# Linear attention feeding an MLP on one core: in which batch k is loaded, and where kv joins the numerators

## The chip, the cores and the metric

The kernel runs on one core of one Trainium2 chip. The metric is device time in microseconds (us), the median of several runs. The engines are named as in the profile: PE is TensorE (matrix products), PEld its weight loads, DVE is VectorE, ACT is ScalarE, POOL is GpSimd, SP is SyncE, which here only issues transfers. Each engine works through its own instructions in program order; engines wait for each other and for transfers (DMA) through semaphores.

## The reference

For 8 batches of 8 heads, 576 positions and head size 64, with phi(x) = elu(x) + 1:

```python
q_p, k_p = phi(q), phi(k)
kv  = einsum('bhsd,bhse->bhde', k_p, v)
z   = sum(k_p, axis=2)
num = einsum('bhsd,bhde->bhse', q_p, kv)
den = einsum('bhsd,bhd->bhs', q_p, z)[..., None] + 1e-06
attn = num / den
# heads side by side: x is 4608 x 512
h = x @ w_in                      # 512 -> 2048
g = h / (1 + exp(-beta * h))
out = g @ w_out                   # 2048 -> 512
```

All inputs and the output are float32. The kernel converts to bf16 on load or in the engines.

## The kernel before, in words

Each batch has nine rows of 64 positions (J = 9) per head. Eight of them make four tiles of 128 positions for the MLP; the ninth, the odd one, goes with the odd rows of all other batches into a last block, xT_tail. So the MLP runs nine times over 512 positions: b = 0 to 7 for the batches and b = 8 for the tail.

One MLP pass has two phases. `h_phase(b)` makes 16 groups (FC = 16): each is four matmuls `x @ w_in` into one PSUM bank (L454, in h_mm) and one silu on ScalarE that writes g (L462). The banks come from `mmps`, a pool of four; a fifth group can start only when the first silu has read its bank. `y_phase(b)` makes four tiles of 128 positions: 16 matmuls each (L472, in y_mm), a copy to SBUF on VectorE (L245) and two stores (L487).

The attention of later batches is laid between these matmuls by hand. Two dictionaries, `sh` and `sy`, hold for each pass what is emitted after group ff of the h phase and after quarter 4t + i of the y phase; `at(sh, 8, f)` adds f after group 8. In the pass b, n = b + 1 is the batch whose x is made ready, and m = b + 2 the one whose phi is made. The emission order is the order in which every engine executes its share, so an instruction that must wait holds up all later ones of its engine.

The pieces, with their profile lines:

- `load_q`, `load_k` (L83) are issued by GpSimd; `load_v` (L83) by SP. Inputs rotate over three buffers (xq, xk: batch mod 3) or two (vf). `load_q(b, after)` is held until the transfer `after` has landed: this is the DMA transpose of phi(q) of the batch before, so that the loads don't take the queues from it. What GpSimd has behind a held load waits too.
- `phi_exps` runs two exps on ScalarE (L144), one for each pair of heads; `phi_rest` the max and the min on VectorE (L148, L155); `phi_all` both. Exp and Silu are in different tables, so each change between them is an ACT_TABLE_LOAD.
- `v_copies` (L173, GpSimd) puts v as bf16 beside a column of ones.
- kv is 72 small matmuls (L184). `kv_both(b)` gives them a PSUM tile of their own (from numps, two buffers) and one copy to SBUF (L239). `numers(b, after)` makes the numerators and denominators of batch b (L309), divides (norms, L392 and L383), and with `after` set first puts kv of batch `after` into free columns of the same PSUM tiles and copies it at the end (L342).
- `q_trans_dma` (L275), `x_trans_dma` (L442 for the four tiles, L446 for the odd row) are transposes by DMA, issued by SP. The first matmul of a h phase needs all four of x.
- `q_odd_trans` (L284) transposes the odd row of phi(q) of batches 0 and 1 on TensorE and copies it on ScalarE (L288). In the pass b = 1 its PSUM tile comes from numps, and the two groups 3 and 4 of that pass also use tiles of numps.

In the kernel before, in the pass b = 1, k of batches 3 and 4 are both loaded early in the h phase, k of batch 5 in the y phase; phi(k) of batch 3 is made in the y phase, and the exps of k of batch 4 at its end. From the pass b = 2 on one pattern holds: kv of batch m goes with `numers(n, m)`, its phi_rest and v_copies are in the h phase, and the exps of the k after it are at step 10 of the y phase.

Of the kernel before, what the change touches and what calls it, by code (L numbers as in the profile page):

```python
# [9 lines left out]
BF16 = mybir.dt.bfloat16  # L10
# [6 lines left out]
def kernel(  # L17
# [12 lines left out]
    B, H, S, D = q.shape  # L30
# [4 lines left out]
    FC = DFF // P  # L35
# [44 lines left out]
    def load(eng, dst, src, b, h0=0, n=4):  # L80

        rows = src[b].rearrange("h (g j) d -> (h g) (j d)", j=J)
        return eng.dma_start(  # L83
            out=dst[:, h0 : h0 + n].rearrange("p h j d -> p h (j d)"),
            in_=rows.rearrange("(i p) e -> p i e", p=P)[:, h0 : h0 + n],
        )
# [84 lines left out]
    def v_copy(eng, b, pr):  # L171
        src = vb[b % 2] if b == 2 else vf[b % 2]
        eng.tensor_copy(  # L173
            vaug[b % 2][:, pr, :, :, 0:D], src[:, places(b, pr)].rearrange("p h j d -> p j h d")
        )
# [51 lines left out]
    def num_tile(name):  # L227
        return numps.tile([P, 2, 512], F32, tag="num", name=name)

    def kv_pair(b, pr, dst):  # L230
        k_quads(b, pr, dst, lambda r, j, h: vaug[b % 2][r, pr, j, h, 0:EA])

    def kv_both(b):

        t = num_tile("kvp")
        for pr in range(2):
            kv_pair(b, pr, [t[:, hh, pr * EA : (pr + 1) * EA] for hh in range(2)])
        st[b, "kvd"] = work.tile([P, 2, 2 * EA], BF16, tag="kv_bd", name="kvd")
        nc.vector.tensor_copy(st[b, "kvd"], t[:, :, 0 : 2 * EA])  # L239
# [40 lines left out]
    def q_odd_trans(b, tp):  # L280

        tv = tp.rearrange("p (a n) -> p a n", a=2)
        for pr in range(2):
            nc.tensor.matmul(  # L284
                tv[:, pr], st[b, "q"][:, pr, J - 1, :], identity,
                is_transpose=True, start=True, stop=True, skip_group_check=True,
            )
        nc.scalar.copy(  # L288
            q_odd[b].rearrange("p (i a) g -> p a i g", i=2),
            tv.rearrange("p a (i g) -> p a i g", i=2),  # L290
        )
# [11 lines left out]
    def quads(b, dst, e, stat, hh, pr):  # L303

        for c in range(2):
            p, j = stat(c)
            for h in range(2):
                r = slice(h * D, (h + 1) * D)
                nc.tensor.matmul(  # L309
                    dst[h][c * G : (c + 1) * G, e * EA : (e + 1) * EA],  # L310
                    st[b, "qTd"][r, (hh * 2 + p) * J + j, :],
                    st[b, "kvd"][r, hh, p * EA : (p + 1) * EA],
                    start=True, stop=True, skip_group_check=True,
                )

    def numer_tile(b, dst, t, prs=(0, 1), e0=0):
        for pr in prs:
            for hh in range(2):
                e = e0 + 2 * (pr - prs[0]) + hh
                quads(b, dst, e, lambda c, pr=pr: (pr, 2 * t + c), hh, pr)  # L320

    def numers(b, after=None):

        pairs = [num_tile("nps") for _ in range(2)]
        odd = [mm_tile("nps_m") for _ in range(2)]
        if after is not None:
            for pr in range(2):
                kv_pair(after, pr, [pairs[pr][:, hh, 6 * EA : 7 * EA] for hh in range(2)])
        for k in range(2):
            dst = [pairs[k][:, h] for h in range(2)]  # L330
            numer_tile(b, dst, k)
            numer_tile(b, dst, 2, (k,), 4)
        numer_tile(b, odd, 3)
        for hh in range(2):
            quads(b, odd, 4 + hh, lambda c: (c, J - 1), hh, None)
        st[b, "nps"] = pairs, odd
        for k in range(3):
            norms(b, k)
        if after is not None:
            st[after, "kvd"] = work.tile([P, 2, 2 * EA], BF16, tag="kv_bd", name="kvd")  # L340
            for pr in range(2):
                nc.vector.tensor_copy(  # L342
                    st[after, "kvd"][:, :, pr * EA : (pr + 1) * EA],
                    pairs[pr][:, :, 6 * EA : 7 * EA],
                )
# [39 lines left out]
    def norms(b, k):  # L385

        den = work.tile([P, 2, 6], F32, tag="den", name="den")
        rden = work.tile([P, 2, 6], F32, tag="rden", name="rden")
        pairs, odd = st[b, "nps"]
        if k < 2:  # L390
            nv = pairs[k][:, :, 0 : 6 * EA].rearrange("p h (n e) -> p h n e", e=EA)
            nc.vector.tensor_scalar(den, nv[:, :, :, D], 1e-6, None, ALU.add)  # L392
            nc.vector.reciprocal(rden, den)
            x = xs_tile(b, k).rearrange("p (h n) d -> p h n d", h=2)
            scale(x, nv[:, :, 0:4, 0:D], rden[:, :, 0:4])
            if k == 0:
                xs_tile(b, 2)
            x = st[b, "xs", 2].rearrange("p (h n) d -> p h n d", h=2)
            scale(x[:, :, 2 * k : 2 * k + 2], nv[:, :, 4:6, 0:D], rden[:, :, 4:6])
            return  # L400
        nv = [a[:, 0 : 6 * EA].rearrange("p (n e) -> p n e", e=EA) for a in odd]
        for h in range(2):
            nc.vector.tensor_scalar(den[:, h], nv[h][:, :, D], 1e-6, None, ALU.add)
        nc.vector.reciprocal(rden, den)
        x = xs_tile(b, 3)
        for h in range(2):
            scale(x[:, 4 * h : 4 * h + 4], nv[h][:, 0:4, 0:D], rden[:, h, 0:4])
        x = xs_tile(b, 4)
        for h in range(2):
            scale(x[:, 2 * h : 2 * h + 2], nv[h][:, 4:6, 0:D], rden[:, h, 4:6])  # L410
# [55 lines left out]
    def mm_tile(name):  # L466
        return mmps.tile([P, 512], F32, tag="mm", name=name)
# [21 lines left out]
    def load_q(b, after):  # L489
        if b < B:  # L490
            hold(load(nc.gpsimd, xq[b % NX], q, b), after)

    def load_k(b):
        if b < B:
            load(nc.gpsimd, xk[b % NX], k, b)

    def load_v(b):
        if b < B:
            load(nc.sync, vf[b % 2], v, b)

    def phi_exps(b, a):
        for pr in range(2):
            phi_part(b, a, pr, xin(b, a, pr))

    def phi_rest(b, a):
        phi_tile(b, a)
        for pr in range(2):
            phi_relu(b, a, pr, xin(b, a, pr))
        for pr in range(2):
            phi_min(b, a, pr)  # L510

    def phi_all(b, a):
        phi_exps(b, a)
        phi_rest(b, a)

    def v_copies(b):
        for pr in range(2):
            v_copy(nc.gpsimd, b, pr)
# [318 lines left out]
    def at(side, n, *fs):  # L837
        side.setdefault(n, []).extend(fs)
# [3 lines left out]
    for b in range(1, B + 1):  # L842
        n = b + 1
        m = n + 1
        sh, sy = {}, {}
        if b == 1:
            at(sh, 0, lambda: q_trans_dma(2))
            at(sh, 1, lambda: v_copies(2))
            at(sh, 2, lambda: load_q(3, st[2, "qTd", "dma"]), lambda: load_k(3))
            at(sh, 2, lambda: load_v(3), lambda: load_k(4))  # L850
            at(sh, 6, lambda: q_odd_trans(1, num_tile("qop")[:, 0].bitcast(BF16)[:, 0:256]))
            at(sh, 8, lambda: kv_both(2))
            at(sy, 1, lambda: numers(2))
        elif n < B:
            if b == 2:
                at(sh, 8, odd_numers, odd_norms, lambda: kv_both(3))
                at(sh, 9, lambda: [x_trans_dma(i, 4) for i in range(2)])
            if m < B:
                at(sh, 2, lambda: phi_rest(m, "k"))
                at(sh, 6, lambda: v_copies(m))  # L860
            at(sh, FC - 1, lambda: numers(n, m if m < B else None))
        if n < B:
            for t in range(NT):
                at(sy, t // 3 + (2 if b == 1 else 0), lambda t=t: x_trans_dma(n, t))
        if m < B:
            at(sy, 3, lambda: phi_all(m, "q"))
            at(sy, 5, lambda: q_trans_dma(m), lambda: load_q(m + 1, st[m, "qTd", "dma"]))
            at(sy, 5, lambda: load_k(m + 2))
            if b == 1:
                at(sy, 4, lambda: v_copies(3))  # L870
                at(sy, 8, lambda: phi_all(3, "k"))
            at(sy, 9, lambda: load_v(m + 1))
            if m + 1 < B:
                at(sy, 10, lambda: phi_exps(m + 1, "k"))
        h_phase(b, xT[b % 3] if b < B else xT_tail, sh)
        y_phase(b, sy, last=(b == B))
# [30 lines left out]
```

## Time and profile before

| | before |
|---|---|
| median of 3 runs | 285.83 us (285.32 to 286.75) |
| span of the profiled execution | 285.3 us |
| TensorE busy | 275.2 us (96%) |
| ScalarE busy | 160.6 us (56%) |
| VectorE busy | 107.8 us (38%) |
| GpSimd busy | 37.3 us (13%) |
| mean over the span | 144 GB/s in 51723 packets |

Busy time counts the instructions' own durations, matmul ends are modelled, and a busy share over the whole span doesn't say where an engine waits. In the timeline, the pass b = 1 begins its h phase at about 49 us and its y phase at 64; the pass b = 2 at 80 and 97; the pass b = 3 at 110.5 and 126. A row gives start, length, engine, line, operation, output and input, the number of instructions merged (x4), and in brackets how long the engine was idle before and what ended that. A wait for several semaphores is put down to the one that came last by the profile, which can name the wrong one. SPq is SP's issuing of transfers.

### The profile page before, as it was taken

How to read it: one execution, taken by the hardware profiler on the slowest of the kernel's cores; microseconds unless marked ns; L12 is line 12 of the kernel's file. 1: busy time of each engine (PE TensorE's matmuls, PEld its weight loads, DVE VectorE, ACT ScalarE, POOL GpSimd, SP SyncE). 2: the span in 40 equal slices, each digit the busy share in tenths (PEclk: the TensorE clock that was granted, in tenths of full speed). 3: DMA queues.
4: the chain of work that ended last, by engine and by line, in shares of the span. 5: the costliest groups of instructions: out<-in, count | busy, mean ns of one | idle time of the engine just before them, and what ended most of it. 6: DMA issues, size and time to landing. Idle time of an engine off the chain costs nothing.

```text
span 285.3 us, 5983 instructions
## 1 busy us (share of the span) xinstructions
PE 275.2 (96%) x2482; PEld 139.1 (49%) x2512; DVE 107.8 (38%) x260; ACT 160.6 (56%) x219; POOL 37.3 (13%) x51
## 2 busy tenths in 40 slices
PE   7799999999989999999999999999999999999994
PEld 2574457444834544454445444544444444444443
DVE  5832578806732464037403840281025100110012
ACT  4878586973776942785288617831860186028500
POOL 8732100314013000320040003000000000000000
PEclk9999999999999999999999999999999999999999
DMA  7999999489969829983997369335403510230032
GB/s 217 205 213 390 249 262 224 109 190 233 199 137 288 141 65 162 269 153 67 162 276 126 80 155 274 56 80 136 99 3 79 117 37 0 57 80 12 0 74 75
DMA packets 51723, 41.03 MB, mean 144 GB/s; under 512 B 31584, under 2 KB 43120, under 8 KB 51696
## 3 DMA queue, kind: packets, MB, share of 16 engines
q1 hardware_dynamic: 38800, 23.61, 34.5%
q0 software_dynamic: 12736, 16.91, 30.1%
q8 instruction: 19, 0.31, 0.5%
q10 hardware_dynamic: 160, 0.13, 0.2%
q14 instruction: 8, 0.07, 0.1%
HBM read 36.71 MB, written 9.44 MB: 162 GB/s over the span
## 4 chain that ended last, share of the span: by engine, by line
PE 91%; DMA 3%; POOL 1%; ACT 1%; issue 1%; DVE 0%; POOLq 0%; ACTq 0%
PE y_ps L472 44%; PE h_ps L454 41%; DMA w_in<-in_moe_w_in_dram 3%; PE nps L184 1%; PE h_ps L665 1%; ACT g L462 1%; PE nps L309 1%; POOL vf L83 1%; PE kvp L184 0%; PE nps_m L309 0%; POOL xk L83 0%; PE nps L563 0%; PE nps L265 0%; PE tp L655 0%; PE zt L194 0%
## 5 line engine op out<-in xcount | busy, mean ns | idle before, releaser
L462 ACT ACTIVATE g<-h_ps,beta_c 128x512 bf16<-128x512 f32 x144 | 97.8, 689 | 89.2 <-PE h_ps L454 88.8
L472 PE MATMUL y_ps<-w_out,g 128*128 128x512 bf16 (+4 forms) x621 | 126.5, 359 | 0.9 <-issue 0.2
L454 PE MATMUL h_ps<-xT,w_in 128*128 128x512 bf16 x486 | 108.5, 379 | 1.9 <-DVE r L148 1.3
L472 PEld LDWEIGHTS <-g 128*128 128x128 bf16 x636 | 60.9, 98 | 61.1
L454 PEld LDWEIGHTS <-w_in 128*128 128x128 bf16 x560 | 54.4, 98 | 66.5 <-issue 1.7
L245 DVE COPY y_sb<-y_ps 128x512 f32<-128x512 f32 (+2 forms) x37 | 24.9, 673 | 81.1 <-PE y_ps L472 81.1
L392 DVE TENSOR_SCALAR den<-nps 128x12 f32<-128x12 f32 x12 | 2.0, 165 | 63.5 <-PE nps L309 63.5
L144 ACT ACTIVATE e<-xk 128x1152 bf16<-128x1152 bf16 x16 | 17.8, 1153 | 2.3 <-DMA xk<-in_k_dram 2.3
L83 POOL DMA_DIRECT2D xq<-in_q_dram x7 | 5.2, 748 | 90.4 <-DMA qTd<-phi_q 44.8
L144 ACT ACTIVATE e<-xq 128x1152 bf16<-128x1152 bf16 x14 | 15.6, 1155 | 0.1
L454 PE MATMUL h_ps<-xT_tail,w_in 128*128 128x512 bf16 x62 | 13.9, 379 | 0.1
L173 POOL CAST vaug<-vf 128x1152 bf16<-128x1152 f32 x10 | 11.2, 1148 | 18.0 <-DMA vf<-in_v_dram 13.5
L155 DVE TENSOR_TENSOR phi_q<-e,r 128x1152 bf16<-128x1152 bf16 (+2 forms) x17 | 11.7, 719 | 2.7 <-ACT e L144 2.4
L155 DVE TENSOR_TENSOR phi_k<-e,r 128x1152 bf16<-128x1152 bf16 x16 | 12.5, 808 | 0.1
L383 DVE TENSOR_TENSOR xs<-nps,rden 128x512 bf16<-128x512 f32 (+1 forms) x24 | 12.3, 552 | 0.4
L144 ACT ACT_TABLE_LOAD x6 | 7.7, 1283 | 6.7 <-DMA xq<-in_q_dram 6.7
L133 PE MATMUL warm_ps<-xT 128*128 128x512 bf16 x20 | 7.5, 530 | 1.8 <-DVE xT L96 1.5
L462 ACT ACT_TABLE_LOAD x6 | 7.7, 1283 | 0.1
L83 POOL DMA_DIRECT2D xk<-in_k_dram x9 | 6.8, 757 | 4.5 <-DMA g<-in_moe_w_out_dram 1.8
L148 DVE TENSOR_SCALAR r<-xq 128x1152 bf16<-128x1152 bf16 x14 | 6.8, 520 | 1.0 <-DMA xq<-in_q_dram 1.0
L184 PEld LDWEIGHTS <-phi_k 64*64 64x64 bf16 x576 | 5.6, 106 | 3.1 <-issue 2.1
L730 DVE TENSOR_SCALAR w_out<-g,rbeta 128x512 bf16<-128x512 f32 x8 | 3.8, 537 | 8.2 <-DMA g<-in_moe_w_out_dram 8.2
(98 smaller groups left out, 119.5 us busy)
## 6 DMA issues: line engine op xcount, KB each, us to landing
out_dram<-y_sb SPq DMA_DIRECT2D x70, 128.0 KB, 2.5
vf<-in_v_dram SPq DMA_DIRECT2D x5, 1152.0 KB, 6.4
xq<-in_q_dram POOLq DMA_DIRECT2D x7, 576.0 KB, 10.0
xk<-in_k_dram POOLq DMA_DIRECT2D x7, 576.0 KB, 12.4
w_in<-in_moe_w_in_dram POOLq DMA_DIRECT2D x4, 512.0 KB, 12.5
g<-in_moe_w_out_dram POOLq DMA_DIRECT2D x2, 1024.0 KB, 17.4
stage<-in_moe_w_out_dram POOLq DMA_DIRECT2D x2, 1024.0 KB, 20.5
stage<-in_q_dram SPq DMA_DIRECT2D x2, 576.0 KB, 4.4
```

The source lines that it names most:

```text
L83: return eng.dma_start(out=dst[:, h0 : h0 + n].rearrange("p h j d -> p h (j d)"), in_=rows.rearrange("(i p) e -> p i e", p=P)[:, h0 : h0 + n],
L133: nc.tensor.matmul(warm_ps[:, 0:cols], warm[:, 0:P], warm[:, 0:cols], start=True, stop=True)
L144: nc.scalar.activation(st[b, a, pr, "e"][:, :, j0:j1], x[:, :, j0:j1], ACTF.Exp)
L148: nc.vector.tensor_scalar(r, x, 0.0, 1.0, ALU.max, ALU.add)
L155: nc.vector.tensor_tensor(st[b, a][:, pr, j0:j1].rearrange("p j (h d) -> p j h d", h=2), st[b, a, pr, "e"][:, :, j0:j1].rearrange("p h j d ...
L173: eng.tensor_copy(vaug[b % 2][:, pr, :, :, 0:D], src[:, places(b, pr)].rearrange("p h j d -> p j h d"))
L184: nc.tensor.matmul(dst[hh][c], st[b, "k"][r, pr, j, c], mov(r, j, h), start=(j == 0), stop=(j == J - 1), skip_group_check=True,)
L245: eng.tensor_copy(dst, src)
L383: nc.vector.tensor_mul(out, num, rd[..., None].to_broadcast(list(num.shape)))
L454: nc.tensor.matmul(hp[:, c0:c1], w_in_sb[ff // 4][:, kc, (ff % 4) * P : (ff % 4 + 1) * P], x[:, kc, c0:c1], start=(kc == 0), stop=(kc == K ...
L462: nc.scalar.activation(g_sb[b % 2][:, ff, :], hp, ACTF.Silu, scale=beta_c[:, ff : ff + 1])
L472: nc.tensor.matmul(yp[:, c0:c1], g_sb[b % 2][:, ff, t * P : (t + 1) * P], w_out_sb[i][:, c, c0:c1], start=(ff == 0), stop=(ff == FC - 1), ...
```

## The change

kv of batch 4 gets a kv_both of its own in the h phase of the pass b = 3, in place of a share of numers(3) in the pass b = 2; the pattern with `after` holds from batch 5 on. k of batch 4 is loaded in the y phase of the pass b = 1 behind q of batch 4, in place of the h phase of that pass; its phi and v_copies go to the y phase of the pass b = 2. It is for a lighter load on the DMA queues in the pass b = 1, where x of batch 2 is transposed. The load of k of batch 5 is now in the pass b = 2, behind q of batch 5; its exps stay at step 10 of that pass's y phase. The odd row of phi(q) of batch 1 is transposed after group 7 in place of group 6.

```diff
@@ the pass b = 1, h phase
-            at(sh, 2, lambda: load_v(3), lambda: load_k(4))
-            at(sh, 6, lambda: q_odd_trans(1, num_tile("qop")[:, 0].bitcast(BF16)[:, 0:256]))
+            at(sh, 2, lambda: load_v(3))
+            at(sh, 7, lambda: q_odd_trans(1, num_tile("qop")[:, 0].bitcast(BF16)[:, 0:256]))
@@ n < B, b > 1
-            if m < B:
+            if b == 3:
+                at(sh, 8, lambda: kv_both(4))
+            if 4 < m < B:
                 at(sh, 2, lambda: phi_rest(m, "k"))
                 at(sh, 6, lambda: v_copies(m))
-            at(sh, FC - 1, lambda: numers(n, m if m < B else None))
+            at(sh, FC - 1, lambda: numers(n, m if 4 < m < B else None))
@@ m < B
             at(sy, 3, lambda: phi_all(m, "q"))
             at(sy, 5, lambda: q_trans_dma(m), lambda: load_q(m + 1, st[m, "qTd", "dma"]))
-            at(sy, 5, lambda: load_k(m + 2))
-            if b == 1:
-                at(sy, 4, lambda: v_copies(3))
-                at(sy, 8, lambda: phi_all(3, "k"))
+            if b < 3:
+                at(sy, 5, lambda: load_k(m + 1))
+                at(sy, 4, lambda: v_copies(m))
+                at(sy, 8, lambda: phi_all(m, "k"))
+            if b > 1:
+                at(sy, 5, lambda: load_k(m + 2))
             at(sy, 9, lambda: load_v(m + 1))
-            if m + 1 < B:
+            if 4 < m + 1 < B:
                 at(sy, 10, lambda: phi_exps(m + 1, "k"))
```

## The prediction

> **What bounds the kernel now.** I read the busy shares on the page first, then TensorE's waits, then the timeline around each wait and around the place where the change puts work, and last the times to landing of the transfers concerned. Page, parts 1 and 4:
>
> ```profile
> PE 275.2 (96%) x2482; PEld 139.1 (49%) x2512; DVE 107.8 (38%) x260; ACT 160.6 (56%) x219; POOL 37.3 (13%) x51
> ...
> PE 91%; DMA 3%; POOL 1%; ACT 1%; issue 1%; DVE 0%; POOLq 0%; ACTq 0%
> ```
>
> TensorE sets the end: nothing is won but by removing its gaps, and any new gap is lost in full. The view of who waited for whom, TensorE alone, has two gaps after the first 15 us:
>
> ```profile
> PE h_ps L454 <- DVE r L148: 1.3, 1, 1.3
> ...
> PE qop L284 <- ACT g L462: 0.4, 1, 0.4
> ```
>
> The timeline shows where they are, and what engines do at the start of batch 3's h phase (columns: start, length, then what, with the idle time before it in brackets):
>
> ```profile
> 1.46 5.92 PE L133 MATMUL warm_ps<-xT 128*128 128x512 bf16 x15 [1.46 <-DVE xT L96]
> ...
> 52.99 4.16 ACT L462 ACTIVATE g<-h_ps,beta_c 128x512 bf16<-128x512 f32 x7
> ...
> 55.47 0.27 PE L284 MATMUL qop<-identity,phi_q 128*128 128x128 bf16 x2 [0.39 <-ACT g L462]
> ...
> 73.89 1.66 SPq L442 DMA_TRANSPOSE xT<-xs  x1
> ...
> 80.33 7.93 PE L454 MATMUL h_ps<-xT,w_in 128*128 128x512 bf16 x35 [1.25 <-DVE r L148]
> ...
> 95.24 0.85 PE L184 MATMUL nps<-vaug,phi_k 64*64 64x65 bf16 x72
> ...
> 99.47 2.20 ACT L144 ACTIVATE e<-xk 128x1152 bf16<-128x1152 bf16 x2
> ...
> 101.69 1.28 ACT L462 ACT_TABLE_LOAD   x1
> ...
> 107.78 2.80 SPq L275 DMA_TRANSPOSE qTd<-phi_q  x2
> ...
> 110.50 13.98 PE L454 MATMUL h_ps<-xT,w_in 128*128 128x512 bf16 x63
> 111.56 0.69 ACT L462 ACTIVATE g<-h_ps,beta_c 128x512 bf16<-128x512 f32 x1 [8.59 <-PE h_ps L454]
> ...
> 114.51 0.75 POOL L83 DMA_DIRECT2D xq<-in_q_dram  x1 [22.22 <-ACT g L462]
> 115.25 0.76 POOL L83 DMA_DIRECT2D xk<-in_k_dram  x1
> ```
>
> See in it: the exps of k of batch 5 run at 99.47, eleven microseconds before ScalarE is needed again at 111.56; and the loads of q of batch 5 and k of batch 6 are issued at 114.51 and 115.25, after batch 3's h phase has begun. That is harmless here, because what they bring is wanted a batch later. Times to landing, first of the x transpose issued at 73.89, then of the k load issued at 115.25:
>
> ```profile
> DMA to landing us min/median/max: 6.4/6.4/6.4
> ```
>
> ```profile
> L83 POOL DMA_DIRECT2D xk<-in_k_dram x1: 760/760/760, 115.2 to 115.2; - x1
> DMA to landing us min/median/max: 12.1/12.1/12.1
> ```
>
> The first corrects a name: 73.89 + 6.4 = 80.29, and TensorE starts at 80.33. The gap of 1.25 us put down to DVE's r is a wait for the last transpose of x of batch 2. In later batches the same transposes land 2.3 us after issue; here k of batches 3 and 4 fills the queues (their loads, issued at 63.6 and 64.4, land at about 72.7 and 76.8).
>
> **What the Trainium skill says.** "DMA: Bandwidth & Descriptors", "Queues, rings and completion order": descriptors of one queue row are consumed in ring order, and an engine takes turns between rows. The trace agrees: q3, k3 and k4, issued 0.75 us apart from GpSimd, land in that order at 69.2, 72.7 and 76.8, and transposes from the other queue get slow beside them. "Perfetto Trace Analysis", "Tensor Engine Instruction": ScalarE, VectorE and GpSimd are strict FIFOs. The trace agrees in that no engine's order departs from the source. "ScalarE: Activation LUTs", "What ACT_TABLE_LOAD costs": 1283 ns for the load; the trace has 1.28 us. "TensorE: Matmul & The Clock Gate", "What's actually happening": after about 3.4 us idle TensorE goes to half clock until it has been busy for about as long. The trace's granted clock shows 1.00 throughout, but the first 15 warm-up matmuls take 5.92 us, 0.39 us each, against 13.8 us for 64 (0.216 each) in an h phase; so it fits.
>
> **The change part by part.**
> 1. q_odd_trans one group later. Its transpose waits until the fourth silu of batch 1 is done: ScalarE starts these at 52.99 and goes on every 0.59, so it is done at 55.47, and TensorE had been ready since 55.08. After the change group 7 (0.86 us) runs first, its bank free since the second silu, and the transpose comes at about 55.95, with nothing to wait for. ScalarE's 0.41 us copy lies beside matmuls. Gain 0.4.
> 2. k of batch 4 no longer loaded at 64.4. Its last share of the queues (72.7 to 76.8) falls away, so the last x transpose, issued near 73.5, lands between 2.3 us (later batches) and about 5 us later, at 75.8 to 78.5; TensorE wants it at 79.07 - 0.39 = 78.7. Gain 1.25, or 1.65 with part 1. ScalarE also drops two exps and VectorE four operations there; both are off the path.
> 3. k of batch 4 is now loaded behind q of batch 4, exactly where k of batch 5 was (issued 85.37, landed 13.5 later, 98.9). Its exps come at the eighth step of batch 2's y phase, after those of q at 97 to 99.5. In time.
> 4. kv of batch 4: 72 small matmuls (0.78 in the chain) leave the numerators of batch 3 and come back after group 8 of batch 3's h phase (0.64 for the like of batch 3). Net -0.1; one VectorE copy in place of two is hidden.
> 5. k of batch 5. This is the part that counts. The old code loads it in batch 1 (m + 2 = 5). The new code has, in batch 1, load_k(4) alone, and in batch 2 load_k(5), both after load_q; but the exps of k of batch 5 stay at the tenth step of batch 2's y phase. So load_k(5) stands on GpSimd behind load_q(5), which is held until the transpose of phi(q) of batch 4 has landed. That is the 114.51 of the trace, and k5 takes the place that k6 had at 115.25. On ScalarE the two exps of k5 stand ahead of the table load and of all silus of batch 3.
>    The working: all that leads to 114.51 follows batch 3's numerators (VectorE's xs, four x transposes, two tail transposes, two stores, the qTd transposes, back to back on the SP queue), and moves earlier by 1.65 (parts 1, 2) + 0.78 (part 4) = 2.43. q5 is issued at 112.08, k5 0.74 later at 112.82. Nothing shows k5 itself here, so I take k6's 12.1 us to landing, the same place beside the same v load and stores: 124.9. Bounds: 9.1 us (k3, second of three loads) and 13.5 (k5 in the old place). Then two exps 2.22, table load 1.28, first silu 0.69: 129.1.
>    TensorE begins the h phase at 110.66 - 2.43 = 108.23, fills its four banks in 4 x 4 x 0.216 = 3.45 us, and from 111.68 waits for the first silu. The gap is 129.1 - 111.68 = 17.4. Queued behind it on TensorE is all that remains; VectorE also stands at phi_rest(5), but batch 2's last store is ahead of that. Silus come every 0.59 against TensorE's 0.86 a group, so it waits once.
> 6. The gap is long enough for the half clock. Bounds 0 and about 3.4: the warm-up row gives 15 x (0.39 - 0.216) = 2.6; the skill's 3.4 to 4 us at half speed would lose 1.7 to 2. I take 2.0.
>
> Sum: 285.8 - 1.65 - 0.1 + 17.4 + 2.0 = 303.5. Later batches load k as before, with the exps a batch behind.
>
> **Rivals.**
> - k5 comes in time or costs nothing. Then only parts 1, 2 and 4 count: 285.8 - 1.75 = 284.1, faster by 0.6%. For it: everything else in the change is on the good side. Against: it needs k5 by about 104, ten microseconds before its queue is released at all; it would take a hold on q5 that ends far earlier than 114.51 shows.
> - The hold ends sooner and the load is quick: phi(q) of batch 4 is ready on VectorE at 104.83, and the SP queue may pass the transposes a few microseconds earlier with emptier queues (the second x transpose of batch 3 takes 2.35 us on the queue against 1.2 elsewhere). With 4 us less before issue and a 9.1 us landing the gap is 10.4, the total 296.5.
> - k5 shares the queues with k6 rather than going ahead of it. Each further load cost 3.5 to 4 us in the row q3, k3, k4, so k5 would land up to 4 us later, and the total is near 307.5. Against: those three landed one after the other.
>
> **How the numbers follow.** The forecast's case gets 0.80, the in-time case 0.04, the short wait 0.08, the shared queue 0.08. Inside the main case: landing 9.1 instead of 12.1 gives -3, a small cold loss -1.5, together 299.0; landing 13.5 gives +1.4, a cold loss of 3.4 +1.4, an SP queue that moves only by 1.65 another +0.8, together 307.1. The range 299.0 to 307.0 leaves out the in-time case and most of the short waits, and parts of the shared queue. Slower has all but the in-time case: 0.95 with 0.01 for no change.
>
> **What would show it right or wrong.** Right: on TensorE a single gap of about 17 us in the h phase of batch 3, after its fourth group, between about 112 and 129; on ScalarE a wait for the DMA of xk ahead of the exps, ending near 125; GpSimd issuing xq, xk, xk near 112 to 114; no gap at 79 to 80 and none at qop; matmuls of 0.43 us spacing after the gap. Wrong: k5 landed before 105, the gap at the head of batch 2 still there, or a clock that does not drop. A total under 288 would refute part 5.

## The result, and the profile after

| | before | changed |
|---|---|---|
| median (range, runs) | 286.29 us (285.32 to 286.88, 4) | 303.56 us (301.93 to 304.28, 4) |
| ratio to before | | 1.0599, 95% interval 1.0543 to 1.0655 |
| TensorE busy | 275.2 us (96%) | 277.7 us (92%) |
| span of the profiled execution | 285.3 us | 302.5 us |

The change makes the kernel 17.3 us slower. Ratios, here and below, leave out the four slow runs, over 1.5% above the fastest of their kernel (three of the kernel before, one of e2); medians are over all runs. On the page after it, TensorE's busy time is only 2.5 us longer, the granted clock has a dip, and a load has come into the chain that ended last. These are TensorE, the clock and the transfers by slices of 7.6 us, the chain by engine, and the chain's lines:

```profile
PE   7899999999999960199999999999999999999995
...
PEclk9999999999999996579999999999999999999999
DMA  8999999499499389700379737913801430131022
...
PE 81%; DMA 9%; DVE 4%; ACT 2%; SPq 2%; issue 2%; POOL 0%; DVEq 0%; POOLq 0%; ACTq 0%
PE h_ps L454 38%; PE y_ps L472 37%; DMA xk<-in_k_dram 4%; DMA xT_tail<-xs 3%; SPq L446 1%; DMA qTd<-phi_q 1%; DMA stage<-in_q_dram 1%; ACT e L144 1%; PE h_ps L665 1%; PE nps L184 1%; DVE phi_q L155 1%; PE kvp L184 1%; DVE r L148 1%; PE nps L309 1%; DVE y_sb L245 1%
```

Read the columns, not the sums: in slices 15 to 17 TensorE has 6, 0, 1 tenths, and the transfers have 8, 9, 7; in the next two, with TensorE back at 9, they have 0. Transfers are under way while TensorE stands still, and the queues are empty when it is at work again. The waits of TensorE and of ScalarE, each in its own view (total, times, longest):

```profile
PE h_ps L454 <- ACT g L462: 16.8, 1, 16.8
```

```profile
ACT e L144 <- DMA xk<-in_k_dram: 23.7, 4, 22.3
```

Neither of the two old gaps is there: no wait at qop, none at the head of pass 2. In their place is one wait for a silu, and on ScalarE one for k. The timeline of the changed kernel gives the whole of it:

```profile
105.33 2.80 SPq L275 DMA_TRANSPOSE qTd<-phi_q  x2
...
107.39 3.62 PE L454 MATMUL h_ps<-xT,w_in 128*128 128x512 bf16 x16
...
111.04 0.75 POOL L83 DMA_DIRECT2D xq<-in_q_dram  x1 [19.71 <-DMA qTd<-phi_q]
111.78 1.49 POOL L83 DMA_DIRECT2D xk<-in_k_dram  x2
...
123.51 2.22 ACT L144 ACTIVATE e<-xk 128x1152 bf16<-128x1152 bf16 x2 [22.26 <-DMA xk<-in_k_dram]
...
125.75 1.28 ACT L462 ACT_TABLE_LOAD   x1
...
127.04 2.42 ACT L462 ACTIVATE g<-h_ps,beta_c 128x512 bf16<-128x512 f32 x4
127.78 6.99 PE L454 MATMUL h_ps<-xT,w_in 128*128 128x512 bf16 x20 [16.77 <-ACT g L462]
```

From the top: phi(q) of batch 4 is transposed; 16 matmuls fill four banks and TensorE stops at 111.01; the transposes have landed, so GpSimd may issue q5, and behind it k5 and k6; ScalarE has waited 22.3 us for k5 when it starts the exps, loads the silu table, and does four silus in a row; after the first, TensorE goes on. Its next 20 matmuls take 6.99 us where 4.48 would do (e9 below). The granted clock is the last column but two (DMA share and GB/s are last) in the stretches before, in and after the gap:

```profile
107.60:111.01 3.41, 3.41 (x16) 1.46 (x15) 0.69 (x1) 0.00 (x0) 0.00 (x0) 1.00 0.81 194
111.01:127.78 16.77, 0.00 (x1) 0.00 (x0) 2.35 (x4) 4.24 (x5) 4.47 (x5) 0.64 0.97 209
127.78:130.00 2.22, 2.22 (x6) 0.84 (x6) 0.00 (x0) 2.00 (x4) 0.00 (x0) 0.50 0.00 0
130.00:132.85 2.85, 2.85 (x8) 0.93 (x7) 0.00 (x0) 1.06 (x2) 0.00 (x0) 0.50 0.00 0
132.85:134.70 1.85, 1.85 (x10) 0.71 (x9) 0.00 (x0) 1.37 (x2) 0.00 (x0) 0.99 0.00 0
```

### The profile page after: what moved, and what is told of

The parts are those of the page before. It is cut to its first block, busy times and chain, and to the rows that moved or that the text cites. A ratio compares the mean times of both kernels' runs of the same rounds, so it can differ in the third digit from the quotient of the medians.

```text
span 302.5 us, 5979 instructions
## 1 busy us (share of the span) xinstructions
PE 277.7 (92%) x2482; PEld 139.7 (46%) x2512; DVE 108.0 (36%) x259; ACT 160.3 (53%) x219; POOL 36.8 (12%) x51
## 4 chain that ended last, share of the span: by engine, by line
PE 81%; DMA 9%; DVE 4%; ACT 2%; SPq 2%; issue 2%; POOL 0%; DVEq 0%; POOLq 0%; ACTq 0%
PE h_ps L454 38%; PE y_ps L472 37%; DMA xk<-in_k_dram 4%; DMA xT_tail<-xs 3%; SPq L446 1%; DMA qTd<-phi_q 1%; DMA stage<-in_q_dram 1%; ACT e L144 1%; PE h_ps L665 1%; PE nps L184 1%; DVE phi_q L155 1%; PE kvp L184 1%; DVE r L148 1%; PE nps L309 1%; DVE y_sb L245 1%
## 5 line engine op out<-in xcount | busy, mean ns | idle before, releaser
L462 ACT ACTIVATE g<-h_ps,beta_c 128x512 bf16<-128x512 f32 x144 | 97.5, 689 | 84.8 <-PE h_ps L454 84.3
L454 PE MATMUL h_ps<-xT,w_in 128*128 128x512 bf16 x486 | 111.3, 385 | 17.4 <-ACT g L462 16.8
L454 PEld LDWEIGHTS <-w_in 128*128 128x128 bf16 x560 | 55.0, 99 | 83.7 <-issue 20.6
L155 DVE TENSOR_TENSOR phi_q<-e,r 128x1152 bf16<-128x1152 bf16 (+2 forms) x17 | 12.5, 765 | 2.7 <-ACT e L144 2.4
L148 DVE TENSOR_SCALAR r<-xk 128x1152 bf16<-128x1152 bf16 x16 | 6.7, 457 | 15.2 <-DMA xk<-in_k_dram 15.2
L155 DVE TENSOR_TENSOR phi_k<-e,r 128x1152 bf16<-128x1152 bf16 x16 | 11.6, 750 | 0.6 <-ACT e L144 0.6
```

What stands on the lines that cost most here:

```text
L148: nc.vector.tensor_scalar(r, x, 0.0, 1.0, ALU.max, ALU.add)
L155: nc.vector.tensor_tensor(st[b, a][:, pr, j0:j1].rearrange("p j (h d) -> p j h d", h=2), st[b, a, pr, "e"][:, :, j0:j1].rearrange("p h j d ...
L454: nc.tensor.matmul(hp[:, c0:c1], w_in_sb[ff // 4][:, kc, (ff % 4) * P : (ff % 4 + 1) * P], x[:, kc, c0:c1], start=(kc == 0), stop=(kc == K ...
L462: nc.scalar.activation(g_sb[b % 2][:, ff, :], hp, ACTF.Silu, scale=beta_c[:, ff : ff + 1])
```

## The experiments

The theory is that of the prediction: k5 is late because its load stands behind the held load of q5, and the silus stand behind its exps. Rivals were that the moved phi and kv of batch 4 overload an engine, that the queues are slow, that k6 takes k5's bandwidth, and, for the matmuls after the gap, that their slowness is not the clock. Ratios are to the kernel before on the same chip, whose medians were 286.75 us beside e1 to e4, 286.84 beside e5 to e8 and 286.32 beside e9 to e11.

| run | median us | ratio, 95% interval |
|---|---|---|
| e1_k5_old_place | 284.85 | 0.9933 (0.9907 to 0.9958) |
| e2_qodd_alone | 287.02 | 1.0023 (1.0001 to 1.0044) |
| e3_k5_ahead_of_q5 | 284.97 | 0.9942 (0.9919 to 0.9966) |
| e4_busy_in_gap | 303.07 | 1.0578 (1.0538 to 1.0618) |
| e5_after_again | 304.03 | 1.0614 (1.0568 to 1.0660) |
| e6_busy_f32 | 302.90 | 1.0565 (1.0529 to 1.0601) |
| e7_k5_exps_late | 291.92 | 1.0190 (1.0146 to 1.0235) |
| e8_load_alone | 285.71 | 0.9965 (0.9951 to 0.9979) |
| e9_busy_longer | 301.57 | 1.0536 (1.0508 to 1.0563) |
| e10_no_k6_behind | 303.33 | 1.0596 (1.0563 to 1.0630) |
| e11_after_beside | 303.14 | 1.0586 (1.0556 to 1.0616) |

**Is it k5's place?** In e1 only GpSimd's order differs from the changed kernel:

```diff
             if b < 3:
-                at(sy, 5, lambda: load_k(m + 1))
+                if b == 1:
+                    at(sy, 5, lambda: load_k(4))
...
-            if b > 1:
-                at(sy, 5, lambda: load_k(m + 2))
+            at(sy, 5, lambda: load_k(m + 2))
```

> The changed kernel with k of batch 5 loaded where it was before, in the y phase of pass 1, now behind k of batch 4; nothing else differs. Theory (the wait for k5 behind the held q5 is the whole loss): the gap of 16.8 us in the h phase of pass 3 and the slow matmuls after it vanish, and what is left is the good side of the change, about 284.2 us, 1.7 under the kernel before; ScalarE may wait 1 to 2 us for k5 in the y phase of pass 2, in idle time. Rival (moving phi of k4 into the y phase of pass 2 and kv of batch 4 into the h phase of pass 3 loads ScalarE or VectorE too much): these stay, so a gap of several us stays at the head of pass 3, and the time stays above 290 us.

Measured 284.85 us. The gap and the slow matmuls are gone, with phi and kv of batch 4 where the change put them. So those cost little, and the rival falls: by the timelines of e1 and before, pass 3 from its first h matmul to its first y matmul became 0.85 us longer (16.14 against 15.29), and pass 2 was 0.70 shorter (15.64 against 16.34). k5 is now third in its queue and lands 15.8 us after issue at 84.3; ScalarE's timeline in e1 shows why that is early enough:

```profile
97.13 2.20 ACT L144 ACTIVATE e<-xk 128x1152 bf16<-128x1152 bf16 x2
100.60 2.22 ACT L144 ACTIVATE e<-xk 128x1152 bf16<-128x1152 bf16 x2 [1.27 <-DVE phi_q L155]
102.83 1.28 ACT L462 ACT_TABLE_LOAD   x1
108.53 0.69 ACT L462 ACTIVATE g<-h_ps,beta_c 128x512 bf16<-128x512 f32 x1 [4.41 <-PE h_ps L454]
```

The second pair are the exps of k5; after the table load ScalarE is idle for 4.41 us until TensorE has its first group.

**The hold or the queues?** e3 swaps two issues:

```diff
+            if b == 2:
+                at(sy, 5, lambda: load_k(5))
             at(sy, 5, lambda: q_trans_dma(m), lambda: load_q(m + 1, st[m, "qTd", "dma"]))
             if b < 3:
-                at(sy, 5, lambda: load_k(m + 1))
+                if b == 1:
+                    at(sy, 5, lambda: load_k(4))
```

> The changed kernel with two loads of pass 2 in the other order: k of batch 5 is issued by GpSimd before the held q of batch 5. Theory (the hold on q5, not the queues' speed, makes k5 late): k5 is issued as soon as GpSimd is done with v of batch 4, near 91 us, lands by about 104, the gap in pass 3 is below 1 us, total about 284.5. Rival (k5 is slow because the pass is full of transfers): it is issued earlier but lands only a few us earlier than 123.5, gap over 8 us, total over 293.

Measured 284.97. GpSimd's timeline in e3:

```profile
91.20 0.75 POOL L83 DMA_DIRECT2D xk<-in_k_dram  x1
110.30 0.74 POOL L83 DMA_DIRECT2D xq<-in_q_dram  x1 [18.35 <-DVE phi_k L155]
111.03 0.75 POOL L83 DMA_DIRECT2D xk<-in_k_dram  x1
```

k5 is the first of them, issued at 91.20 and landed 9.7 us later, at 100.9; TensorE has no wait in these passes. (The releaser named in the second row is the view's guess; the hold is on the transpose.) So two issues in the other order are worth 18.6 us, the difference of the medians of e3 and the changed kernel. k5 is issued 20.6 us sooner than at 111.78, and its transfer is 2.0 us quicker (9.7 against 11.7): the hold makes k5 late, and the speed of its transfer is a small part.

**Does k6 share?** e10 takes the load of k6 from behind k5:

```diff
-            if b > 1:
+            if b > 2:
                 at(sy, 5, lambda: load_k(m + 2))
...
             if b == 3:
+                at(sh, 7, lambda: load_k(6))
                 at(sh, 8, lambda: kv_both(4))
```

> The changed kernel with the load of k of batch 6 moved from behind k of batch 5 to pass 3, after group 7; so k5 is the last load in its queue. Theory (loads of one queue are served in order): k5 lands as before, 11.7 us after its issue, and the time stays at 303 to 304. Rival (k5 shares the queues with k6): k5 lands 2 us or more earlier, and the time falls by as much, to 301.5 or less.

Landing of k5 in e10:

```profile
L83 POOL DMA_DIRECT2D xk<-in_k_dram x1: 750/750/750, 112.8 to 112.8; - x1
DMA to landing us min/median/max: 11.6/11.6/11.6
```

11.6 us, against 11.7 in the changed kernel's first profile and 11.4 in e11, both with k6 behind it, and 303.33 us against 303.14 in e11. The edit moves k6 less far than it seems to, because GpSimd does not wait for group 7. Its timeline in e10:

```profile
112.83 0.75 POOL L83 DMA_DIRECT2D xk<-in_k_dram  x1
117.62 2.24 POOL L173 CAST vaug<-vf 128x1152 bf16<-128x1152 f32 x2 [4.04 <-DMA vf<-in_v_dram]
119.80 0.75 POOL L83 DMA_DIRECT2D xk<-in_k_dram  x1
```

k6 is issued 7 us behind k5 in place of 0.75, and the two still overlap until k5 lands at 124.4. Had k6 taken a share, 7 us without it should show in k5's landing, and nothing does; a run with no k6 at all was not made.

**Is it ScalarE's order?** In e7 k5 is as late as ever, but its exps stand behind the silus of pass 3:

```diff
             if 4 < m < B:
-                at(sh, 2, lambda: phi_rest(m, "k"))
+                if b == 3:
+                    at(sh, FC - 1, lambda: phi_all(5, "k"))
+                else:
+                    at(sh, 2, lambda: phi_rest(m, "k"))
...
-            if 4 < m + 1 < B:
+            if 5 < m + 1 < B:
                 at(sy, 10, lambda: phi_exps(m + 1, "k"))
```

> The changed kernel with the exps and the max and min of k of batch 5 moved from the end of pass 2 to the end of pass 3's h phase, behind its silus; the late load of k5 is left as it is. Theory (the loss comes from the silus queued on ScalarE behind the exps that wait for k5): group 4 of pass 3 no longer waits, TensorE instead waits for phi of k5 ahead of kv of batch 5 at the end of that h phase, from about 122 to 126, 4 us and perhaps 1 of clock, total about 289.5, between 288 and 291. Rival (a late k5 costs the same wherever its exps stand): over 300.

Measured 291.92, above the range expected, far below the rival. The timeline of e7:

```profile
122.33 0.69 ACT L462 ACTIVATE g<-h_ps,beta_c 128x512 bf16<-128x512 f32 x1 [0.18 <-PE h_ps L454]
123.99 1.28 ACT L144 ACT_TABLE_LOAD   x1 [0.97 <-DMA xk<-in_k_dram]
...
125.28 2.22 ACT L144 ACTIVATE e<-xk 128x1152 bf16<-128x1152 bf16 x2
126.48 0.76 DVE L155 TENSOR_TENSOR phi_k<-e,r 128x1152 bf16<-128x1152 bf16 x1 [1.63 <-ACT e L144]
...
127.29 0.71 PE L184 MATMUL nps<-vaug,phi_k 64*64 64x65 bf16 x36 [5.00 <-DVE phi_k L155]
```

The silus run through and TensorE waits 5.0 us at kv of batch 5. I had the table load done before k5 lands; it carries the wait for the load itself, so 1.28 us stand behind the landing. And the 5 us gap was enough for the half clock, which the windows of e7 show at 0.50 and 0.53 from 127.29 to 132.0. Against e5, the changed kernel beside it, e7 is 12.1 us faster. So of some 18.6 us that the late load costs (e3), about 12 come from what was queued behind it on ScalarE.

**The half clock.** e4 fills the gap with matmuls whose result nothing reads:

```diff
+    def keep_busy(n):
+        t = num_tile("busy")
+        for _ in range(n):
+            nc.tensor.matmul(
+                t[:, 0], xT[0][:, 0, 0:P], xT[0][:, 0, :], start=True, stop=True,
+                skip_group_check=True,
+            )
...
             if b == 3:
+                at(sh, 3, lambda: keep_busy(66))
                 at(sh, 8, lambda: kv_both(4))
```

> The changed kernel with 66 extra matmuls of 128x512 on TensorE after group 3 of pass 3, into a PSUM tile that nothing reads; they fill about 14.3 of the 16.8 us in which it waits. Theory (the clock drop costs 2.5 us beside the gap): group 4 still starts when the first silu is done, near 127.8, but its matmuls are 0.216 us apart and the total is 2.5 us below the changed kernel, about 301. Rival (the matmuls after the gap are slow for another reason, such as the silus): no gain, 303.5.

The cause is shown by the trace of e4: the wait for the first silu ends about where it did (127.15, against 127.78), and the next matmuls run at full clock. A row of its timeline, and one of its windows:

```profile
127.15 4.48 PE L454 MATMUL h_ps<-xT,w_in 128*128 128x512 bf16 x19 [1.84 <-ACT g L462]
```

```profile
127.15:129.00 1.85, 1.80 (x8) 0.87 (x9) 0.00 (x0) 1.85 (x4) 0.00 (x0) 1.00 0.05 9
```

The time was not: 303.07. The profiled execution of e4 has a wait of 1.25 us "for issue" amid the numerators of pass 4 that the changed kernel lacks; what causes it was not settled. e6 therefore uses 16 float32 matmuls in place of 66 bf16 ones (stage in place of xT), and e5 runs the changed kernel beside it.

> As e4_busy_in_gap, but the gap is filled by 16 float32 matmuls of 128x512 instead of 66 bf16 ones with their weight loads, so that TensorE has hardly any instructions more. Theory (the clock drop costs 2.5 us, and e4 gave half of it back in a 1.25 us wait for instructions in pass 4 that its profile shows): 2.5 us under the changed kernel beside it, about 301. Rival (the 2.5 us are mostly not there to gain): within 1 us of the changed kernel.

> The changed kernel itself once more, to have it beside the next run on one chip: 303 to 304 us, 1.06 of the kernel before; a gap of about 17 us before group 4 of pass 3 and about 5 us of matmuls at 0.427 us spacing after it.

302.90 against 304.03: the intervals overlap, and the profile of e6 says why the gain is small. The fillers end 2.46 us before the first silu is done, and the clock fell all the same, though only once TensorE was back at work. Windows of e6, from the end of the fillers on:

```profile
124.96:127.42 2.46, 0.00 (x0) 0.00 (x0) 0.90 (x2) 2.43 (x4) 0.00 (x0) 1.00 0.13 23
127.42:129.00 1.58, 1.58 (x5) 0.64 (x5) 0.00 (x0) 1.58 (x4) 0.00 (x0) 0.63 0.00 0
129.00:131.00 2.00, 2.00 (x6) 0.76 (x5) 0.00 (x0) 1.02 (x3) 0.00 (x0) 0.50 0.00 0
```

e9 has 18 of them, with e11, the changed kernel, beside it.

> As e6_busy_f32 with 18 float32 matmuls in place of 16: at 0.869 us each they fill 15.6 us, so that under 1.5 us of the gap are left, against 2.5 in e6, where the granted clock still fell to 0.50 for some 3 us. Theory (the half clock after the gap costs 2.5 us): clock 1.00 throughout, matmuls 0.216 us apart after the gap, 2 to 2.5 us under the changed kernel beside it. Rival (the end of the gap moves or the time is lost again later): within 1 us of the changed kernel.

> The changed kernel, for comparison on the same chip: 303 to 304 us.

TensorE after the fillers of e9:

```profile
127.13 4.48 PE L454 MATMUL h_ps<-xT,w_in 128*128 128x512 bf16 x20 [0.18 <-ACT g L462]
```

The wait for the silu is 0.18 us, the 20 matmuls take 4.48 us at a clock of 1.00, and the median is 301.57 against 303.14: 1.6 us, less than expected, with intervals that barely touch (1.0508 to 1.0563, and 1.0556 to 1.0616). Not all of it need be the clock's: by the profiles this row starts 19.25 us after the head of pass 3 in e9, and 19.78 in e11. The loss by the clock differs between executions: the same 20 matmuls took 6.99 us in the changed kernel's first profile, 6.37 in e11, 6.10 in e5 and 5.82 in e10, so 2.5, 1.9, 1.6 and 1.3 us over 4.48.

**The two gains, one without the other.** e2 is the kernel before with the odd row's transpose after group 7; e8 is e1 with it after group 6:

```diff
-            at(sh, 6, lambda: q_odd_trans(1, ...))
+            at(sh, 7, lambda: q_odd_trans(1, ...))
```

> The kernel before with only the transpose of the odd row of phi(q) of batch 1 moved from group 6 to group 7. Theory: the gap of 0.39 us at the transpose goes, the gap of 1.25 us at the head of pass 2 stays or grows by what TensorE gains, because it ends when the last x transpose lands: between -0.4 and 0 us against the kernel before, 285.9 to 286.3. Rival (the two gaps are independent): -0.4 with the second gap unchanged at 1.25.

> e1_k5_old_place without the move of the odd row's transpose, which stays after group 6: k of batch 4 loaded late and all that goes with it, k5 in its old place. Theory: the gap of 0.4 us at the transpose is back and is lost in full, because the head of pass 2 no longer waits: 0.4 over e1, about 285.2. Rival (TensorE arrives later at pass 2 and loses nothing, or the gap at its head comes back): equal to e1, or over 286.

e2 measured 287.02: no gain, 0.27 over the kernel before and just outside what was expected (0.4 under to equal). Its runs spread from 286.2 to 291.0, so I read no loss from it. The first h matmuls of passes 1 and 2 in the kernel before start at 48.86 and 80.33. Those of e2, and the landing of its last x transpose, issued at 72.96:

```profile
48.34 7.08 PE L454 MATMUL h_ps<-xT,w_in 128*128 128x512 bf16 x31
...
79.50 7.93 PE L454 MATMUL h_ps<-xT,w_in 128*128 128x512 bf16 x35 [1.48 <-DVE r L148]
```

```profile
DMA to landing us min/median/max: 6.4/6.4/6.4
```

The gap at qop is gone and the one at the head of pass 2 has grown from 1.25 to 1.48: counted from the head of pass 1, TensorE came 0.55 us sooner and the transpose landed about 0.4 sooner. So part of the gain is taken back. From the head of pass 1 to that of pass 2 there are 31.16 us in e2 and 31.47 before, 0.31 less in one profile of each, which the time does not show. e8 measured 285.71, and the gap at qop is back:

```profile
55.38 0.27 PE L284 MATMUL qop<-identity,phi_q 128*128 128x128 bf16 x2 [0.39 <-ACT g L462]
```

That is 0.86 over e1 by the medians, on two chips. From head to head the profiles have 30.17 us in e8 and 29.65 in e1: the transpose is worth about 0.5 beside the late load of k4, and the late load 1.3 alone. By the ratios that is 0.4% for the load alone and 0.7% together with the transpose.

## Why the prediction was right

The forecast was 303.5 us. By its own steps, on the trace after:

1. The transpose of the odd row: forecast 0.4. The wait at qop is gone. Alone it brings no time that can be seen (e2), beside part 2 about 0.5 by the profiles of e8 and e1. The part gives its 0.4 without that condition; the sum takes the two together.
2. The load of k4: forecast 1.25. The last x transpose, issued at 72.61, lands 2.4 us later, as in later batches, and TensorE does not wait. The first h matmuls of pass 1 before (those of pass 2 start at 80.33), then of passes 1 and 2 after:

```profile
48.86 6.22 PE L454 MATMUL h_ps<-xT,w_in 128*128 128x512 bf16 x27
```

```profile
48.38 7.08 PE L454 MATMUL h_ps<-xT,w_in 128*128 128x512 bf16 x31
...
77.89 7.93 PE L454 MATMUL h_ps<-xT,w_in 128*128 128x512 bf16 x35
```

   From head to head there are 29.51 us after against 31.47 before: 1.96 for both parts, where 1.65 was forecast. The 0.3 more is in the way the view counts: idle time runs from the modelled end of the matmul before, but where nothing waits the next row starts ahead of that end. In the changed kernel the y matmuls of pass 1 run from 65.94 for 12.11 us, to 78.05, and the row at 77.89 starts 0.16 sooner. So each of the two gaps was 0.16 longer than the view gives it. In time, e1 is 1.9 under the kernel before beside it. That the wait put down to VectorE's r was for the transfer is not separated by these runs, since the change takes this r away too; but these matmuls read only xT and w_in, and in the kernel before and in e2 they start within 0.2 us after the last x transpose lands.
3. k4 behind q4: in time, as forecast, but barely; it landed 14.6 us after issue, and ScalarE waited 0.63 us for it.
4. kv of batch 4: forecast 0.1 to win. By e1, pass 2 won 0.70 and pass 3 lost 0.85, so about 0.15 is lost. The 72 matmuls were priced at 0.78 where they stood and 0.64 where they went; where they went, they take 0.73.
5. k5: the forecast had it issued at 112.82, landed at 124.9, the first silu done at 129.1 and a gap of 17.4 us. Measured 111.78, 123.5, 127.7 and 16.8. Pieces of the chain that ended last, after the change:

```profile
91.72 7.59 DMA xT_tail<-xs
...
106.72 3.76 DMA qTd<-phi_q
...
111.78 11.65 DMA xk<-in_k_dram
```

   The 12.1 us taken from k6 became 11.7. The second transpose of phi(q) of batch 4 landed 3.8 us after its issue, where the trace before had 5, so q5 was released a microsecond sooner. TensorE's stop also came sooner, at 111.01 against 111.68, so the gap shrank by only 0.6. Of that 0.67, 0.48 was there before the change could act, since pass 1 began at 48.38 in place of 48.86. The route to the hold was not the one told: the divisions of batch 3 on VectorE began 3.14 us sooner (93.71 against 96.85), where the forecast moved all by 2.43; then VectorE waited 2.94 us, in place of 0.94, until the odd-row transposes let it write xs. The qTd transposes thus began 2.45 sooner. That this agrees with 2.43 is luck: two differences cancel. e1 and e3 show that this load's place is the whole loss.
6. The half clock: forecast 2.0, measured 2.5 by the matmuls in the first profile, 1.3 to 1.9 in others, and at most 1.6 by time in e9. After the gap the granted clock does read 0.50. The warm-up row, from which the forecast took a bound of 2.6, is weaker support than it was given: its matmuls are slow while the granted clock reads 1.00.

That the total is within 0.1 us of the measured median is luck in part: the median before was 285.8 for the forecast and became 286.29 with one run more, and the rise is 17.3 where the sum has 17.65. The mechanism and the large term, the gap, were right by the working; the errors of the small terms go both ways.

The rivals: k5 in time (284.1) is what e1 and e3 make true by moving the load, at 284.85 and 284.97. The hold did end sooner than forecast, but by 1.0 us and not by 4. For the shared queue nothing speaks: k5 landed sooner than the 12.1 us of the forecast, not up to 4 us later, and e10 gained nothing by 7 us without k6. That GpSimd's loads land in the order of their issue is read from their landings: in e11 k5 at 123.1 and k6 at 125.9.

The versions that beat both kernels are e1 and e3, with all of the change except the late load of k5: 0.9933 and 0.9942 of the kernel before, with intervals that overlap.

## What to carry to other kernels

When a load moves in the issue order, look for its first reader and what is queued behind that reader; a wait on an engine that was idle anyway costs nothing until something the bound engine needs stands behind it. A load issued behind a held one inherits the hold, whatever its own needs. And a gain at one wait can be taken back, in whole or in part, by the next wait on the same engine, if that one's end does not move as far: try the two together.

## What the runs showed that was not expected

- In e6, after a gap of 2.46 us on TensorE, the granted clock fell to 0.50; after one of 1.84 us (e4) it did not. The Trainium skill ("TensorE: Matmul & The Clock Gate", "What's actually happening") puts the fall after about 3.4 us of idle time; in e6 TensorE was at work again after less. At the end of the gap the clock was still 1.00, and it fell within the 1.6 us after. In the changed kernel, with its long gap, it was 1.00 for the first 4.0 us and 0.50 from 5.0 us on. In e6 the gap followed float32 matmuls and in e4 bf16 ones, so the length is not the only difference; float32 matmuls alone don't lower the clock, for in e9 it was 1.00 throughout theirs.
- A float32 matmul of 128x512 took 0.87 us (15.61 us for 18 in e9; the trace shows each as two of 0.43), four times the 0.216 of bf16.
- The table load of e7 waited for the input of the exp behind it (until 123.99) and took its 1.28 us after, so it did not hide in the wait.
